# Loading a group's rows two steps before their statistics, taking weight pieces and transform steps by turns, and fetching the remaining rows with six transfers

## The chip, the cores and the metric

The kernel runs on one core of a Trainium2 chip. The core has TensorE (PE, matrix products), VectorE (DVE), ScalarE (ACT), GpSimd (POOL), SyncE (SP, which here only issues transfers) and 16 DMA engines. The metric is the device time of one execution in microseconds. The kernel before takes 1058.84 us, the median of three runs (1058.2 to 1059.17).

## The reference

Three stages follow one another, in float32:

```python
def _attn_ref(q, k, v, tau):                     # batch 4, heads 8, rows 576, head size 64
    scores = scale * np.matmul(q, k.transpose(0, 1, 3, 2))
    thresh = np.max(scores, axis=-1, keepdims=True) - tau
    scores = np.where(scores >= thresh, scores, -1000000000.0)
    ...                                          # softmax over what is left
    return np.matmul(attn, v)

def _moe_ref(x, mu_k, mu_r, w_k, w_v, w_r):      # 4 x 576 x 512, inner size 1024
    xk = mu_k * x + (1.0 - mu_k) * x_prev        # x_prev: x one row later, zeros first
    xr = mu_r * x + (1.0 - mu_r) * x_prev
    k = np.maximum(xk @ w_k, 0.0)
    v = k * k @ w_v
    r = 1.0 / (1.0 + np.exp(-(xr @ w_r)))
    return r * v

def _moe2_ref(x, w_ch1, w_ch2):                  # w_ch1 512 x 2048, w_ch2 2048 x 512
    X = np.fft.fft(x, axis=1)
    X = np.fft.fft(X, axis=2)
    u = x + np.real(X)
    un = (u - mean(u)) / np.sqrt(var(u) + 1e-06)
    return u + np.maximum(un @ w_ch1, 0.0) @ w_ch2
```

The change concerns the third stage.

## The kernel before

The 2304 rows (4 batches of 576) pass the stages as streams that overlap. Attention (to some 508 us) and the second stage (products `kps`, `rps`, `vps`, to some 614 us) work on half a batch at a time. The second stage's output goes through `xnat` to memory as `xd[b]`. The third stage transforms one batch at a time by matrix products with cosine and sine tables, and then runs the two channel products over nine groups of 256 rows.

**Fold.** `fft_fold(b)` loads a batch's rows (`xa`, `xb`, lines 773 and 774; the remaining rows `ra`, `rb` by `load_rem`, lines 777 to 787), and adds and subtracts them in mirrored pairs (`folded`: ACT at lines 792 and 793, DVE at 794 to 797). `ra` holds 98 partitions: the same 32 rows of the batch three times, at partitions 0, 33 and 65, and one more row twice, at 32 and 97; `rb` likewise. A batch takes ten SP transfers for this. **Transform.** `fft_one` and `fft_two` are the products `f` (lines 818 to 821), `fb`, `fz` and `fa`; they store the sum `u` of input and transform as `ud[g]`, two groups for each batch.

**Channel products.** The weights are taken in four quarters. For each group `norm(g)` loads `un` from `ud[g]` (line 995, two transfers of 256 KB), takes mean and variance on DVE (998 to 1009, with a square root on ACT at 1003) and scales on ACT (1011). `turn` transposes it on PE into `ut` (1024), of which ACT writes a high part (1027) and DVE the rest (1028). `ch1` multiplies with `w_ch1` into `c1ps` (1107 to 1109, 12 products of 256 columns for one of four steps f); ACT and DVE make of it the high and low parts `hh` (1119, 1120). `ch2` multiplies with `w_ch2` into `c2ps` (1129 to 1131), and the sum goes into `u` (loaded at 1153, added at 1177, stored at 1178). A later block of `c1ps` takes the buffer of an earlier one once its `hh` is made.

**Weight pieces.** `weight_pieces` loads 256 KB of a weight (`wraw`, line 56, issued on ACT's queue), and DVE and ACT split it into parts for the products (lines 69 to 71, 75, 79). Quarter 1 has 16 pieces.

**The order.** The driver (lines 1233 to 1270) walks over the steps of `mixer()`, (quarter q, group g, step f). For each step it takes so many steps of the generator `behind` as it has credit, two for each of the first groups: in the kernel before all pieces of quarter 1 first, then the transform of batches 2 and 3. `ahead_of` names the group whose `norm` and `turn` are written at step f = 2 of which (q, g). A scheduler then orders each engine's instructions by its own estimate of times and by priorities, so the order in the program is not the order of the code. Transfers issued on SP and ACT share eight semaphores in turn: a transfer waits at its issue until the previous one with its semaphore has landed. The tiles `ra`, `rb`, `un` and `xnat` of the last stream share four buffers of the pool tag "o".

Of the kernel before, what the change touches and what calls it, by code (L numbers as in the profile page):

```python
# [10 lines left out]
F32 = mybir.dt.float32  # L11
# [9 lines left out]
D, FF, FC = 512, 1024, 2048  # L21
# [8 lines left out]
def tile_kernel(ctx: ExitStack, tc: tile.TileContext, a):  # L30
    nc = tc.nc
    pe, dve, act, pool, sp = nc.tensor, nc.vector, nc.scalar, nc.gpsimd, nc.sync
# [5 lines left out]
    xd = [dram.tile([S + 1, D], F32, name=f"xd{b}") for b in range(B)]  # L38
    ud = [dram.tile([128, 2, D], F32, name=f"ud{g}") for g in range(9)]
# [706 lines left out]
    chp = rstack.enter_context(tc.tile_pool(name="chp", bufs=1, side="right"))  # L746
# [30 lines left out]
    def load_rem(b):  # L777

        xa = chp.tile([128, D], F32, tag="o", bufs=4, name="ra")[:98]
        xb = chp.tile([128, D], F32, tag="o", bufs=4, name="rb")[:98]  # L780
        for r in (0, 33, 65):
            sp.dma_start(xa[r:r + 32], xd[b][256:288, :])
            sp.dma_start(xb[r:r + 32], xd[b][544:576, :])
        for r in (32, 97):
            sp.dma_start(xa[r:r + 1], xd[b][576:577, :])
            sp.dma_start(xb[r:r + 1], xd[b][576:577, :])
        return xa, xb

    def folded(xa, xb, n):
# [76 lines left out]
    def fft_fold(b):  # L866
        while written[b] < 2:
            yield
        settle()
        prs = prs_of[b] = load_pairs(b)  # L870
        ra, rb = load_rem(b)
        parts_e, parts_o = [], []
        for xa, xb in prs:
            e, o = folded(xa, xb, 128)
            yield
            parts_e.append(split_tile(e, 257, "fse"))
            parts_o.append(split_tile(o, 256, "fso"))
            yield
        e, o = folded(ra, rb, 98)
        yield  # L880
        ske = stack_tile(e, 257, "ske")
        sko = stack_tile(o, 256, "sko")
        fold_of[b] = (parts_e, parts_o, ske, sko)
        yield

    def fft_one(b):
        parts_e, parts_o, ske, sko = fold_of.pop(b)
        G = [fp.tile([128, 2, 290], F32R, tag=f"G{i}", bufs=1, name=f"G{i}") for i in range(2)]
        Hh = [fp.tile([128, 2, HS], F32R, tag=f"H{i}", bufs=1, name=f"H{i}") for i in range(2)]
        for mc in range(2):  # L890
            o = stage_1(parts_e, ske, tc1, tc1r, 290, 128 * mc, 128 * mc + 128)
            fsplit(G[0][:, mc], G[1][:, mc], o)
            o = stage_1(parts_o, sko, ts1, ts1r, HS, 128 * mc, 128 * mc + 128)
            fsplit(Hh[0][:, mc], Hh[1][:, mc], o)
            yield
        o = stage_1(parts_e, ske, tc1, tc1r, 290, 256, 257)
        fsplit(g1[0:1], g1[32:33], o)
        sl = slice(32 * b, 32 * b + 32)
        act.activation(g1[64:65, sl], o[:, 256:288], AF.Copy)
        dve.tensor_tensor(g1[96:97, sl], o[:, 256:288], g1[0:1, 256:288].bitcast(F32), op=ALU.subtract)  # L900
        for i, x in enumerate((G[0], G[1], Hh[0], Hh[1])):
            act.activation(grem[i][:, :, b, :], x[:, :, 256:288].bitcast(F32), AF.Copy)
        spec[b] = (G, Hh)
        yield

    def fft_two(b):
        G, Hh = spec.pop(b)
        prs = prs_of.pop(b)
        z, _ = stage_2(G, None, 0, 288, 289)
        zr = fp.tile([1, 257], F32, name="zr")  # L910
        act.activation(zr, z[0:1, 0:257], AF.Copy)
        for i in range(2):
            pa, pb = stage_2(G, Hh, 0, 128 * i, 128 * i + 128)
            make_u(2 * b + i, pa, pb, *prs[i], z=zr if i == 0 else None)
            yield
# [12 lines left out]
    def chain(*gens):  # L928
        for g in gens:
            yield from g  # L930


    wq = {}
    SEVEN = (3,)

# [4 lines left out]
    def quarter(q):  # L940

        if q % 2:
            t = [big(f"B{i}", f"cB{i}") for i in range(2)]
            wq[q] = [[x[:, 2048 * k:2048 * k + 2048] for x in t] for k in range(2)]
        else:
            wq[q] = [halves(0, "cA"), None]
        todo = []
        for k, src in enumerate(("w_ch1", "w_ch2")):
            def to(c, n, k=k):
                if wq[q][k] is None:  # L950
                    wq[q][k] = halves(k, "cA")
                return whole(wq[q][k], 2048 * q)(c, n)

            todo += [(a[src], to, 8 * q + j) for j in ((0, 2, 4, 6, 1, 3, 5, 7) if k == 0 else range(8))]
        if q not in SEVEN:
            yield from weight_pieces(todo, None, stage2, 256, rb=3, bb=2, lows=dve if q < 2 else None)
            return
        more[q] = xwp.tile([128, 2, 3, 2, 256], F32R, name=f"more{q}")
        todo = todo[:8] + [(s, to if i % 4 != 1 else lambda c, n: None, 8 * q + i)
                           for (s, to, _), i in zip(todo[8:], (0, 1, 3, 2, 4, 5, 7, 6))]  # L960
        kept = {}

        def less(x, y, to):
            t = spare(F32)
            dve.tensor_tensor(t, x, y, op=ALU.subtract)
            act.activation(to[0], t, AF.Copy)
            pool.tensor_tensor(to[1], t, to[0].bitcast(F32), op=ALU.subtract)
            return t

        def then(k, wf):  # L970
            p, i = divmod(k - 8, 4)
            if k < 8:
                return
            ext = [[more[q][:, p, m, t] for t in range(2)] for m in range(3)]
            if i == 0:
                kept["b11"] = wf
            elif i == 1:
                kept["b12"] = wf
                kept["t1"] = less(wf, kept["b11"], whole(wq[q][1])(1024 * p + 256, 256))
            elif i == 2:  # L980
                less(wf, kept["b12"], ext[1])
                kept["t2"] = less(wf, kept["t1"], ext[0])
            else:
                less(wf, kept["t2"], ext[2])

        yield from weight_pieces(todo, None, stage2, 256, rb=3, bb=2, then=then)


    uts, pairs, hs, more = {}, {}, {}, {}

    def norm(g):

        u = [chp.tile([128, D], F32, tag="o", bufs=4, name="un") for _ in range(2)]
        for j in range(2):
            sp.dma_start(u[j], ud[g][:, j])
        st = chp.tile([128, 32], F32, tag="lnst", bufs=1, name="lnst")
        for j in range(2):
            dve.bn_stats(st[:, 6 * j:6 * j + 6], u[j])
            dve.bn_aggr(st[:, 12 + 2 * j:14 + 2 * j], st[:, 6 * j:6 * j + 6])
        mean, var = st[:, 12:16:2], st[:, 13:16:2]  # L1000
        ve, sd, r0, t0, rstd, nb = (st[:, k:k + 2] for k in (16, 18, 20, 22, 24, 26))
        dve.tensor_scalar(ve, var, 1e-6, None, op0=ALU.add)
        act.activation(sd, ve, AF.Sqrt)
        dve.reciprocal(r0, sd)
        dve.tensor_tensor(t0, r0, r0, op=ALU.mult)
        dve.tensor_tensor(t0, t0, ve, op=ALU.mult)
        dve.tensor_scalar(t0, t0, -0.5, 1.5, op0=ALU.mult, op1=ALU.add)
        dve.tensor_tensor(rstd, r0, t0, op=ALU.mult)
        dve.scalar_tensor_tensor(nb, mean, -1.0, rstd, op0=ALU.mult, op1=ALU.mult)
        for j in range(2):  # L1010
            act.activation(u[j], u[j], AF.Identity, scale=rstd[:, j:j + 1], bias=nb[:, j:j + 1])
        return u
# [191 lines left out]
    for _ in stream:  # L1204
# [9 lines left out]
        if ffn.get("r_done") and len(uts) < 2:  # L1214
            g = len(uts)
# [17 lines left out]
    for _ in cgen:  # L1233
        pass
    behind = chain(
        quarter(1), fft_fold(2), fft_one(2), fft_two(2),
        fft_fold(3), fft_one(3), fft_two(3), fft_last(), done(),
    )

    ahead_of = {(0, 0): 2, (0, 1): 3, (1, 2): 4, (1, 3): 5, (0, 5): 6, (0, 6): 7, (0, 7): 8}  # L1240
    credit = 0.0
    for (q, gs), f in mixer():
        g = gs[-1]
        credit += 2.0 if (q, g) < (0, 4) else 1.25 * len(gs)
        while credit >= 1:
            credit -= 1
            next(behind, None)
        if f == 2 and (q, g) in ahead_of:
            while (q, g) == (0, 5) and not fft_done:
                next(behind)  # L1250
            n = ahead_of[q, g]
            turn(n, norm(n))
        if (q, g) in ((1, 5), (2, 1)) and f == 3:
            for _ in behind:
                pass
            behind = quarter(q + 1)
        if q > 0 and g == 8 and f == 3:
            for _ in behind:
                pass
# [126 lines left out]
```

## Time and profile before

| | |
|---|---|
| median of three runs | 1058.84 us |
| profiled execution | 1057.07 us |
| span of its trace | 1055.0 us |
| TensorE busy | 1004.3 us (95%) |
| VectorE busy | 715.9 us (68%) |
| ScalarE busy | 536.6 us (51%) |
| GpSimd busy | 395.8 us (38%) |
| mean granted clock of TensorE | 0.988 |

TensorE is the engine that is nearly always busy, and 73% of the chain of work that ended last is its own. A share over the whole span says little here: the windows of the stages show where it waited, and the timeline at those places what it waited for. Times of day in the text (as 624.71) are microseconds from the span's start.

### The profile page before, as it was taken

How to read it: one execution, taken by the hardware profiler on the slowest of the kernel's cores; microseconds unless marked ns; L12 is line 12 of the kernel's file. 1: busy time of each engine (PE TensorE's matmuls, PEld its weight loads, DVE VectorE, ACT ScalarE, POOL GpSimd, SP SyncE). 2: the span in 40 equal slices, each digit the busy share in tenths (PEclk: the TensorE clock that was granted, in tenths of full speed). 3: DMA queues.
4: the chain of work that ended last, by engine and by line, in shares of the span. 5: the costliest groups of instructions: out<-in, count | busy, mean ns of one | idle time of the engine just before them, and what ended most of it. 6: DMA issues, size and time to landing. Idle time of an engine off the chain costs nothing.

```text
span 1055.0 us, 18820 instructions
## 1 busy us (share of the span) xinstructions
PE 1004.3 (95%) x6807; PEld 884.6 (84%) x6807; DVE 715.9 (68%) x1880; ACT 536.6 (51%) x1211; POOL 395.8 (38%) x495
## 2 busy tenths in 40 slices
PE   5887889999999999999999988999999999999998
PEld 4565669988998888999799887898998888889997
DVE  6799988667776685865457978556537449236776
ACT  4688767675866757767265734342413113113332
POOL 1545868455574564843233101000014125112231
PEclk9899989999999999999999999999999999999999
DMA  6443331121211212100722656436325435223221
GB/s 223 149 134 86 112 108 60 48 72 38 72 60 54 66 47 72 51 24 14 209 72 88 205 186 200 157 103 226 129 89 184 130 114 179 97 99 122 101 100 61
DMA packets 45636, 114.52 MB, mean 109 GB/s; under 512 B 6319, under 2 KB 6740, under 8 KB 45544
## 3 DMA queue, kind: packets, MB, share of 16 engines
q1 hardware_dynamic: 27920, 74.47, 22.0%
q10 hardware_dynamic: 12344, 22.13, 6.8%
q0 software_dynamic: 5280, 16.72, 4.5%
q8 instruction: 54, 0.88, 0.4%
q14 instruction: 38, 0.31, 0.1%
HBM read 84.98 MB, written 28.32 MB: 107 GB/s over the span
## 4 chain that ended last, share of the span: by engine, by line
PE 73%; DVE 11%; DMA 7%; ACT 4%; issue 3%; POOL 1%; ACTq 0%; SPq 0%; DVEq 0%; POOLq 0%
PE c1ps L1109 6%; PE c1ps L1107 6%; PE c1ps L1108 6%; PE av L388 6%; PE s L227 5%; PE c2ps L1129 4%; PE c2ps L1131 4%; PE c2ps L1130 4%; PE p L1064 4%; PE t L329 4%; PE kps L408 2%; PE vps L536 2%; PE vps L537 2%; PE vps L538 2%; PE kps L409 2%
## 5 line engine op out<-in xcount | busy, mean ns | idle before, releaser
L267 DVE TENSOR_REDUCE small<-s 128x1 f32<-128x576 f32 x144 | 107.0, 752 | 48.1 <-PE s L227 36.9
L1178 POOL DMA_DIRECT2D ud<-u x54 | 29.4, 545 | 268.3 <-DVE u L1177 167.7
L290 POOL TENSOR_SCALAR e<-e,small 128x576 f32<-128x576 f32 x112 | 89.5, 806 | 89.0 <-DVE small L653 74.6
L282 DVE SCALAR_TENSOR_TENSOR e<-s,small,e 128x576 f32<-128x576 f32 x128 | 102.7, 812 | 25.4 <-ACT e L278 22.2
L278 ACT ACTIVATE e<-s,small 128x576 f32<-128x576 f32 x128 | 93.8, 744 | 29.4 <-DVE small L267 27.7
L1119 ACT ACTIVATE hh<-c1ps 128x256 fp32r<-128x256 f32 (+1 forms) x84 | 37.1, 443 | 138.4 <-PE c1ps L1109 114.7
L1120 DVE SCALAR_TENSOR_TENSOR hh<-c1ps,hh 128x256 fp32r<-128x256 f32 (+1 forms) x84 | 41.6, 497 | 86.6 <-ACT hh L1119 86.5
L329 PE MATMUL t<-ident,e 128*128 128x128 f32 x512 | 82.9, 279 | 10.2 <-ACT pt L332 4.6
L332 ACT ACTIVATE pt<-t 128x512 f32<-128x512 f32 x128 | 75.1, 599 | 22.8 <-PE t L329 21.0
L493 POOL TENSOR_TENSOR k<-relu,k 128x288 fp32r<-128x288 f32 x64 | 54.6, 855 | 68.4 <-ACT k L491 64.2
L329 PEld LDWEIGHTS t<-ident,e 128*128 128x128 f32 x512 | 61.6, 142 | 21.3 <-issue 6.5
L408 PE MATMUL kps<-xh,wk 128*128 128x288 f32 x256 | 78.2, 306 | 0.8 <-DVE fdd L851 0.3
L536 PE MATMUL vps<-k,wv 128*128 128x288 f32 x256 | 77.7, 305 | 0.4 <-ACT tg L524 0.4
L537 PE MATMUL vps<-k,wv 128*128 128x288 f32 x256 | 77.4, 303 | 0.0
L538 PE MATMUL vps<-k,wv 128*128 128x288 f32 x256 | 76.8, 301 | 0.0
L1107 PE MATMUL c1ps<-ut,cA 128*128 128x256 f32 (+1 forms) x224 | 71.2, 319 | 5.7 <-DVE hh L1120 4.0
L409 PE MATMUL kps<-xl,wk 128*128 128x288 f32 x256 | 76.3, 298 | 0.0
L410 PE MATMUL kps<-xh,wk 128*128 128x288 f32 x256 | 76.2, 298 | 0.0
L1109 PE MATMUL c1ps<-ut,cB 128*128 128x256 f32 (+1 forms) x256 | 76.0, 297 | 0.0
L1107 PE MATMUL c1ps<-ut,cB 128*128 128x256 f32 (+1 forms) x256 | 75.8, 296 | 0.0
L1108 PE MATMUL c1ps<-ut,cB 128*128 128x256 f32 (+1 forms) x256 | 75.7, 296 | 0.0
L1108 PE MATMUL c1ps<-ut,cA 128*128 128x256 f32 (+1 forms) x224 | 70.8, 316 | 0.2 <-DVE ut L1028 0.2
(273 smaller groups left out, 3117.4 us busy)
## 6 DMA issues: line engine op xcount, KB each, us to landing
u<-ud SPq DMA_DIRECT2D x36, 512.0 KB
wraw<-in_w_ch ACTq DMA_DIRECT2D x64, 256.0 KB
rawqk<-in_qk SPq DMA_DIRECT2D x24, 608.0 KB
ud<-u POOLq DMA_DIRECT2D x54, 256.0 KB, 2.6
v<-in_v SPq DMA_DIRECT2D x16, 320.0 KB
un<-ud SPq DMA_DIRECT2D x18, 256.0 KB
out<-u SPq DMA_DIRECT2D x18, 256.0 KB
wraw<-in_w_k SPq DMA_DIRECT2D x8, 512.0 KB
```

What stands on the lines that cost most here:

```text
L267: dve.tensor_reduce(st[:, 0:1], sps[n][:, :, 0:HS], axis=AX.XY, op=ALU.max, negate=True)
L278: act.activation(two(eview(n)), sps[n][:, :, 0:HS], AF.Exp, bias=st[:, 0:1])
L282: dve.scalar_tensor_tensor(e, sps[n][:, :, 0:HS], st[:, 1:2], e, op0=ALU.is_ge, op1=ALU.mult, accum_out=st[:, 2:3])
L329: pe.transpose(t[:, k, :], e[:, o + 128 * k:o + 128 * (k + 1)], ident)
L408: pe.matmul(ps, wh, x[0][k], start=(k == 0), stop=False)
L409: pe.matmul(ps, wh, x[1][k], start=False, stop=False)
L536: pe.matmul(ps, wv[0][:, c:c + 128], k2[0][:, k, :], start=(k == 0), stop=False)
L537: pe.matmul(ps, wv[0][:, c:c + 128], k2[1][:, k, :], start=False, stop=False)
L538: pe.matmul(ps, wv[1][:, c:c + 128], k2[0][:, k, :], start=False, stop=(k == 7))
L1107: pe.matmul(ps, wh, ut[0][:, k, :], start=(k == 0), stop=False)
L1108: pe.matmul(ps, wh, ut[1][:, k, :], start=False, stop=False)
L1109: pe.matmul(ps, wl, ut[0][:, k, :], start=False, stop=(k == 3))
```

## The change

`load_rem` loads `ra` and `rb` by three transfers each: 64 partitions from one transfer whose source is the same 32 rows read twice (a stride of zero), 32 partitions from another, and the two single rows from a third, whose source is one row read twice. The loads of `un` move out of `norm` into `fetch`, which the driver calls at f = 0 of the same (q, g), and `norm` and `turn` follow at f = 2 (f = 3 for group 2). `by_turns` takes the pieces of quarter 1 and the steps of the transform of batch 2 alternately. Every line behind `by_turns` moves by 17, so `hh` stands at 1136 and 1137 and `bn_stats` at 1015.

```diff
         xa = chp.tile([128, D], F32, tag="o", bufs=4, name="ra")[:98]
         xb = chp.tile([128, D], F32, tag="o", bufs=4, name="rb")[:98]
-        for r in (0, 33, 65):
-            sp.dma_start(xa[r:r + 32], xd[b][256:288, :])
-            sp.dma_start(xb[r:r + 32], xd[b][544:576, :])
-        for r in (32, 97):
-            sp.dma_start(xa[r:r + 1], xd[b][576:577, :])
-            sp.dma_start(xb[r:r + 1], xd[b][576:577, :])
+        for x, r in ((xa, 256), (xb, 544)):
+            rows = xd[b][r:r + 32, :]
+            sp.dma_start(x[33:97], rows.rearrange("(a p) d -> a p d", a=1).to_broadcast([2, 32, D]))
+            sp.dma_start(x[0:32], rows)
+            sp.dma_start(x[32:98:65], xd[b][576:577, :].to_broadcast([2, D]))
         return xa, xb
...
+    def by_turns(*gens):
+        left = list(gens)
+        while left:
+            for g in list(left):
+                try:
+                    next(g)
+                except StopIteration:
+                    left.remove(g)
+                    continue
+                yield
...
+    fetched = {}
+
+    def fetch(g):
+        fetched[g] = [chp.tile([128, D], F32, tag="o", bufs=4, name="un") for _ in range(2)]
+        for j in range(2):
+            sp.dma_start(fetched[g][j], ud[g][:, j])
+
     def norm(g):
 
-        u = [chp.tile([128, D], F32, tag="o", bufs=4, name="un") for _ in range(2)]
-        for j in range(2):
-            sp.dma_start(u[j], ud[g][:, j])
+        if g not in fetched:
+            fetch(g)
+        u = fetched.pop(g)
...
-        quarter(1), fft_fold(2), fft_one(2), fft_two(2),
+        by_turns(quarter(1), chain(fft_fold(2), fft_one(2), fft_two(2))),
...
-        if f == 2 and (q, g) in ahead_of:
+        n = ahead_of.get((q, g))
+        if f == 0 and n:
             while (q, g) == (0, 5) and not fft_done:
                 next(behind)
-            n = ahead_of[q, g]
+            fetch(n)
+        if f == (3 if n == 2 else 2) and n:
             turn(n, norm(n))
```

On SP, where the channel products begin (some 616 us in the kernel before). `ud_67` to `ud_70` are groups 0 to 3, `xd_65` is batch 2. Before:

```order
L1153 DMA u<-ud_67 128x1024
L995 DMA un<-ud_69 128x512
L1153 DMA u<-ud_68 128x1024
L995 DMA un<-ud_69 128x512
L995 DMA un<-ud_70 128x512 x2
L1153 DMA u<-ud_69 128x1024
L782 DMA ra<-xd_65 32x512
L783 DMA rb<-xd_65 32x512
```

After:

```order
L1170 DMA u<-ud_67 128x1024
L783 DMA ra<-xd_65 64x1x512
L784 DMA ra<-xd_65 32x512
L785 DMA ra<-xd_65 2x512
L1170 DMA u<-ud_68 128x1024
L783 DMA rb<-xd_65 64x1x512
L784 DMA rb<-xd_65 32x512
L785 DMA rb<-xd_65 2x512
L1006 DMA un<-ud_69 128x512 x2
L1006 DMA un<-ud_70 128x512 x2
L1170 DMA u<-ud_69 128x1024
```

The remaining rows of batch 2 now go ahead of the loads of groups 2 and 3, which stood around `u1` and ahead of them.

On VectorE, in the same stretch: the rows around the first statistics of group 2. Before:

```order
L69 TENSOR_SCALAR wbits<-wraw 128x256
L70 SCALAR_TENSOR_TENSOR wbits<-wraw,wbits 128x256
L71 SCALAR_TENSOR_TENSOR wbits<-wraw,wbits 128x256
L998 BN_STATS lnst<-un 128x6
L79 TENSOR_TENSOR cB_7703<-wbits,cB_7702 128x256
L1120 SCALAR_TENSOR_TENSOR hh<-c1ps,hh 128x256
L999 BN_AGGR lnst<-lnst 128x2
L79 TENSOR_TENSOR cB_7703<-wbits,cB_7702 128x256
L69 TENSOR_SCALAR wbits<-wraw 128x256
L1120 SCALAR_TENSOR_TENSOR hh<-c1ps,hh 128x256
```

After (the first four `hh` stand ahead of these rows, the fifth is their last):

```order
L79 TENSOR_TENSOR cB_7695<-wbits,cB_7694 128x256
L70 SCALAR_TENSOR_TENSOR wbits<-wraw,wbits 128x256
L793 TENSOR_TENSOR fp<-ra,rb 98x255
L69 TENSOR_SCALAR wbits<-wraw 128x256
L794 TENSOR_TENSOR fq<-rb,ra 98x255
L71 SCALAR_TENSOR_TENSOR wbits<-wraw,wbits 128x256
L1015 BN_STATS lnst<-un 128x6
L70 SCALAR_TENSOR_TENSOR wbits<-wraw,wbits 128x256
L795 TENSOR_TENSOR fy<-fp,fq 98x257
L850 MEMSET fdd 128x1
L1015 BN_STATS lnst<-un 128x6
L1137 SCALAR_TENSOR_TENSOR hh<-c1ps,hh 128x256
```

The statistics (`BN_STATS`) stood ahead of the second `hh`; they now stand behind the fourth and ahead of the fifth, with the fold of the remaining rows (`fp`, `fq`, `fy`) ahead of them.

On TensorE, around the transposes of group 2 (`ut<-ident,un`); `f` is the first transform product of batch 2. Before:

```order
L1130 MATMUL c2ps<-cA_7351,hh 128x512
L1131 MATMUL c2ps<-cA_7350,hh 128x512 x2
L1024 MATMUL ut<-ident,un 128x128 x8
L1129 MATMUL c2ps<-cA_7350,hh 128x512
L1130 MATMUL c2ps<-cA_7351,hh 128x512
L1129 MATMUL c2ps<-cA_7350,hh 128x512
L1130 MATMUL c2ps<-cA_7351,hh 128x512
L1131 MATMUL c2ps<-cA_7350,hh 128x512 x2
L1107 MATMUL c1ps<-ut_7807,cA_7092 128x256 x2
L1108 MATMUL c1ps<-ut_7808,cA_7092 128x256
```

After:

```order
L1147 MATMUL c2ps<-cA_7343,hh 128x512
L1148 MATMUL c2ps<-cA_7342,hh 128x512 x2
L1041 MATMUL ut<-ident,un 128x128 x8
L1124 MATMUL c1ps<-ut_7847,cA_7084 128x256 x2
L817 MATMUL f_7980<-tc_6209,fseh 128x290
L818 MATMUL f_7980<-tc_6209,fseh 128x290
L819 MATMUL f_7980<-tc_6209,fsel 128x290
L817 MATMUL f_7980<-tc_6209,fseh 128x290
L818 MATMUL f_7980<-tc_6209,fseh 128x290
L819 MATMUL f_7980<-tc_6209,fsel 128x290
L820 MATMUL f_7980<-tc1r,ske 128x290
L817 MATMUL f_7990<-ts_6211,fsoh 128x288
```

The six products `c2ps` that followed the transposes now precede them, and 14 products `f` follow, which stood behind the transposes of group 3.

## Rows read from the trace of the kernel before

**Rows 1.** The page: span.

```profile
span 1055.0 us, 18820 instructions
```

**Rows 2.** Windows by stage: length, busy times, granted clock, DMA share, GB/s.

```profile
505.00:560.00 55.00, 52.38 (x380) 48.11 (x379) 28.95 (x69) 24.09 (x73) 18.74 (x29) 1.00 0.53 159
560.00:616.00 56.00, 54.18 (x405) 51.72 (x404) 49.90 (x151) 37.05 (x96) 11.12 (x11) 1.00 0.40 126
616.00:664.00 48.00, 40.66 (x252) 35.97 (x251) 37.84 (x119) 20.07 (x48) 3.42 (x6) 0.96 0.73 228
664.00:1040.00 376.00, 376.00 (x2329) 334.94 (x2328) 213.56 (x482) 104.51 (x226) 78.65 (x103) 1.00 0.38 126
```

**Rows 3.** Timeline of TensorE, 616 to 662 us: start, length, line, idle before.

```profile
624.71 0.58 PE L1107 MATMUL c1ps<-ut,cA 128*128 128x256 f32 x1 [3.84 <-DVE hh L1120]
...
640.63 1.03 PE L1024 MATMUL ut<-ident,un 128*128 128x128 f32 x8
...
647.69 0.50 PE L1129 MATMUL c2ps<-cA,hh 128*128 128x512 f32 x1 [1.31 <-ACT hh L1119]
...
659.32 0.50 PE L1107 MATMUL c1ps<-ut,cA 128*128 128x256 f32 x2 [1.61 <-ACT ut L1027]
```

**Rows 4.** Windows of 4 us inside that stage.

```profile
620.00:624.00 4.00, 0.87 (x4) 0.38 (x2) 0.70 (x2) 0.38 (x1) 0.00 (x0) 1.00 1.03 404
624.00:628.00 4.00, 3.29 (x15) 3.21 (x16) 2.34 (x8) 0.33 (x2) 0.00 (x0) 0.57 0.81 287
```

**Rows 5.** Timeline of TensorE: products at either level of the clock.

```profile
614.27 0.28 PE L1108 MATMUL c1ps<-ut,cA 128*128 128x256 f32 x1
614.39 0.28 PE L1109 MATMUL c1ps<-ut,cA 128*128 128x256 f32 x1
...
620.25 0.39 PE L1129 MATMUL c2ps<-cA,hh 128*128 128x512 f32 x1
620.48 0.39 PE L1130 MATMUL c2ps<-cA,hh 128*128 128x512 f32 x1
...
625.30 0.41 PE L1109 MATMUL c1ps<-ut,cA 128*128 128x256 f32 x1
625.51 0.41 PE L1107 MATMUL c1ps<-ut,cA 128*128 128x256 f32 x1
```

**Rows 6.** Timeline of VectorE, 612 to 662 us.

```profile
623.30 0.69 DVE L998 BATCH_NORM_STATS2 lnst<-un 128x6 f32<-128x512 f32 x1 [4.50 <-DMA un<-ud]
...
624.23 0.42 DVE L1120 SCALAR_TENSOR_TENSOR hh<-c1ps,hh 128x256 fp32r<-128x256 f32 x1
...
630.30 0.69 DVE L998 BATCH_NORM_STATS2 lnst<-un 128x6 f32<-128x512 f32 x1
...
631.65 0.40 DVE L1120 SCALAR_TENSOR_TENSOR hh<-c1ps,hh 128x256 fp32r<-128x256 f32 x1
...
642.77 0.68 DVE L1028 TENSOR_TENSOR ut<-ut,ut 128x512 fp32r<-128x512 f32 x1
```

**Rows 7.** Chain of waits that ended last, 610 to 662 us.

```profile
616.54 6.74 DMA un<-ud
```

**Rows 8.** Timeline of ScalarE and its queue, 612 to 662 us.

```profile
622.61 0.38 ACT L1119 ACTIVATE hh<-c1ps 128x256 fp32r<-128x256 f32 x1 [2.84 <-DMA u<-ud]
```

**Rows 9.** Timeline of ScalarE and its queue, 500 to 532 us.

```profile
522.80 0.33 ACTq L56 DMA_DIRECT2D wraw<-in_w_ch  x1
523.18 0.21 ACT L793 ACTIVATE fq<-xb 128x2 f32<-128x2 f32 x1 [5.58 <-DMA rb<-xd]
...
529.21 0.19 ACT L793 ACTIVATE fq<-rb 98x2 f32<-98x2 f32 x1
```

**Rows 10.** Timeline of SyncE, 500 to 560 us.

```profile
512.47 0.46 SPq L782 DMA_DIRECT2D ra<-xd  x1
```

**Rows 11.** Timeline of TensorE, 505 to 535 us.

```profile
524.81 0.40 PE L818 MATMUL f<-tc,fseh 128*128 128x290 f32 x1 [0.35 <-ACT fseh L803]
```

**Rows 12.** The page: DMA queue, packets, MB, share of 16 engines.

```profile
q1 hardware_dynamic: 27920, 74.47, 22.0%
```

## The prediction

> **What bounds the kernel now.** I read the page first, for the span [rows 1], then the windows by stage [rows 2], since a share over the whole span hides where TensorE stood still. From 664 to 1040 us TensorE is busy 376.00 of 376.00 us: nothing that the change moves can be gained there, only lost. From 505 to 560 it lacks 2.62 us, from 560 to 616 1.82 us, and from 616 to 664, where the channel products begin, 48.00 − 40.66 = 7.34 us. That last stage is the only one with something to win. Its clock is 0.96, not 1.00.
>
> The timeline of TensorE says where the 7.34 us lie [rows 3]: 3.84 us at 624.71 behind a DVE `hh`, 1.31 us at 647.69 behind an ACT `hh`, 1.61 us at 659.32 behind the `ut` of group 3; 0.58 us are left for smaller ones. I then followed the longest one back. DVE stood idle for 4.50 us and then ran the first `bn_stats` of group 2 at 623.30, because `un` had not landed; the `hh` that TensorE needed stands right behind it in DVE's order and runs at 624.23 [rows 6]. The chain of waits names the same transfer: `un`, issued at 616.54 and 6.74 us long [rows 7]. So DVE did no useful work for an instruction that could have waited, at the head of a queue with one that could not. ACT has its own part in it: its `hh` at 622.61 came after 2.84 us in which a weight load ahead of it waited for the semaphore of `u` [rows 8].
>
> The wait has a second price. In the window 620 to 624 TensorE is busy 0.87 of 4 us, and in the next the granted clock is 0.57 [rows 4]. Products of 256 columns then start 0.21 us apart (625.30, 625.51) where they took 0.12 (614.27, 614.39) [rows 5]: near half of the speed, so the lower of the two levels, 1.2 instead of 2.4 GHz. Twelve products at 0.09 us more are 1.1 us; the next ones of 512 columns add about 0.1. The stage has thus 7.34 + 1.2 = 8.5 us that could go at most.
>
> **The order of `hh` and statistics.** In the changed order the first four `hh` stand ahead of both `bn_stats`, and the waits at 624.71 and the fall of the clock should go: −3.84 − 1.2. What is late next I estimate one by one, from the order and the durations above.
>
> The first `hh` now stands behind one weight piece more on DVE: 0.3 us. The second, on ACT, stands behind two weight loads whose semaphores belong to loads issued shortly before; the row nearest to this is the wait of 2.84 us [rows 8], and nothing excludes 0; I take 0.6, nearer to 0, since a weight load has half of `u`'s bytes.
>
> The fifth `hh` is the critical one. Ahead of it on DVE stand `fp` and `fq`, which need the remaining rows of batch 2, and two `bn_stats`, which need both tiles `un`. TensorE without its two losses would be there about 5.0 us (3.84 + 1.2) earlier than before, less the 0.9 just charged. Before, that `hh` ran from 631.65 to 632.05 [rows 6], and between 624.71 and 640.63 TensorE's timeline has no wait [rows 3], so it was asked for at 632.05 or later; 4.1 us earlier that is 628.0 or later, and I take 629.5. If the six transfers of `ra` and `rb` land like other transfers, `un` lands about 4 us later than the 623.28 of before, near 627 to 628, and the `hh` runs at 629.5 to 631. I take 0.9 us of waiting.
>
> The transposes of group 2 stood at 640.63 [rows 3], 10.3 us behind the second `bn_stats` at 630.30 [rows 6]. Now they ask for a `bn_stats` near 629.5, so stand near 640; TensorE comes there near 638.5, with the six `c2ps` products of 0.23 us [rows 5] already done (1.4 us that stood behind before). Wait: 1.5 us. A cover goes with these six: they hid DVE's low half of `ut`, 0.68 us for each of its two pieces [rows 6]; behind the transposes now stand only two `c1ps`. Wait: 0.7 us. For group 3, whose wait was 1.61 us, I take 0.5, since its loads are issued some steps earlier. The wait at 647.69 came from a full ACT queue behind the late weight pieces; with one piece for each transform step I count it as gone.
>
> Sum of what is left: 0.3 + 0.6 + 0.9 + 1.5 + 0.7 + 0.5 = 4.5 us of 8.5, so the stage gains 4.0 us (2.5 if group 2 waits as much as the whole chain allows, 5.5 if `hh` and transposes come free; 8.5 is the ceiling).
>
> **The six transfers.** 16 issues of some 0.46 us [rows 10] leave SP, with the same bytes. SP is on no path by its own time; what counts is the semaphores. From 517.60 to 523.18 ACT stood 5.58 us behind a weight load that waited for the semaphore of one `ra` transfer, issued at 512.47 and landed at about 522.8 [rows 9, 10]. With fewer transfers that load waits for `xb` and an older weight piece instead, which land earlier; ACT's activations behind it start up to 4 us sooner. TensorE felt little of it: 0.35 us at 524.81 behind ACT [rows 11]. Against this the `fq` of the remaining rows, at 529.21 without a wait [rows 9], stands ahead of an activation for the second stage, and now rests on a transfer of a form that the trace does not have. Bounds for 505 to 616: −1.5 (all waits that ACT ends) to +4 (below); I take −0.3.
>
> How long one such transfer of 128 KB takes no row shows. From below: at 404 GB/s [rows 4] 0.33 us beside others. From above: 10.3 us, what the 64 KB of `ra` took while the DMA engines were full [rows 9, 10]. I take the lower end in the stage at 616, since its `un`, four times the bytes of the old row transfer, took 6.7 us [rows 7] with half a megabyte ahead of it, and keep the upper for the range.
>
> Here the row and a rule part. The rows of this kernel show no transfer that reads its source twice. The Trainium skill (DMA: Bandwidth & Descriptors, "Why a DMA increments its semaphore by 16 and not by 1") says that the number of DMA engines is the largest up to 16 that divides the slowest dimension of both sides; with a source of 2 x 32 rows that would be two engines. By it the time would be that of the first rival.
>
> **From 664 us on** the orders grow alike again, near 790 us, and TensorE is full: 0, with up to +1.5 where a weight piece comes late, since the pieces now end later.
>
> **Sum.** −4.0 − 0.3 = −4.3 us against the profiled execution's 1057.07 (its span of 1055.0 and 2.07 around it): 1052.8. The median of the runs is 1.77 above that execution, so 1058.84 − 4.3 = 1054.5 us. Chance 0.50, own range 1052.5 to 1056.5.
>
> **Rival 1: the 64-row transfers crawl on few engines.** On two of them each has 32 packets of 2 KB. The queue's mean is 0.220 x 16 x 1055 / 27920 = 0.133 us for a packet [rows 12], so 4.3 us for each transfer instead of 0.5 over sixteen, and what follows in the queue (`u`, `un`) waits on those two. `rb` then lands near 629 and the fifth `hh` runs near 631.5: 1.8 us more waiting. In the first stage `fq` comes about 2 us late and holds the activation behind it: 2 us. The gain is 4.3 − 1.8 − 2.0 = 0.5: 1058.3. For it: the source's form. Against it: nothing in the trace. Chance 0.26.
>
> **Rival 2: slower.** The same wait for `rb` of batch 0, but at the price of the full engines: a transfer of 64 KB took 10.3 us there [rows 9, 10]. If `rb` lands after 534, ACT stands at `fq` with the activations of the second stage behind it, and TensorE loses one us for each us beyond 530, where it asks for them. At 5 us and a stage at 616 that gains 2.5 it is 1058.84 + 2.5 = 1061.3. It decides from 535 on, where the loss exceeds what the later stage can give. For it: the 10.3 us. Against: only six transfers are issued where ten were, and the last of the ten landed before 529. Chance 0.14.
>
> **Rival 3: the wait moves.** DVE needs 37.84 of 48 us in the stage [rows 2]; if the `bn_stats` chain with the fold's work in it takes 13 us instead of 10.3, the transposes of groups 2 and 3 give back the 3 us: 4.3 − 3 = 1.3, 1057.5. Chance 0.10.
>
> **How the numbers follow.** A measurement of this kernel tells 0.2%, 2.1 us, from no change. Below 1056.7 counts as faster: 0.46 of the forecast's 0.50, 0.06 of rival 1, 0.03 of rival 3: 0.55. Above 1061.0 slower: 0.10 of rival 2, 0.06 of rival 1, 0.03 of late pieces: 0.19. Between them 0.26. The range reaches from 1051 (ceiling nearly reached) to 1061, just short of rival 2.
>
> **What would show it.** Right: no wait above 2 us in TensorE's timeline from 616 to 664, a clock of 1.00 there, idle time of about 4.5 instead of 7.34 us, and the first `bn_stats` of group 2 behind four `hh`. Rival 1: `ra` and `rb` land some 5 us after their issue and the fifth `hh` waits for them. Rival 2: a wait of several us near 530, before a `kps`, that ACT ends. Wrong altogether: a loss after 664, where I count on full cover.

## The result and the profile after

The changed kernel takes 1073.63 us, the median of four runs (1072.77 to 1075.8), beside 1058.52 for the kernel before: a ratio of 1.0145, 95% interval 1.0128 to 1.0163. It is slower by 15 us where 4.3 us of gain were forecast, and lies above the stated range. Ratios here are of undisturbed runs, so they can differ a little from the quotient of the medians beside them.

The page of the changed kernel, its span, TensorE, and the queue that answers to [rows 1, 12]:

```profile
span 1072.3 us, 18786 instructions
...
PE 1010.1 (94%) x6807; PEld 889.7 (83%) x6807; DVE 713.2 (67%) x1880; ACT 535.3 (50%) x1211; POOL 396.5 (37%) x495
...
q1 hardware_dynamic: 27680, 74.47, 21.8%
```

The same 74.47 MB go through the queue. Of the 17.3 us that the span grew, 5.8 are in TensorE's busy time (1004.3 before, with as many instructions: products at the lower clock), the rest is waiting. The windows by stage that answer to [rows 2] (length, busy times with counts, granted clock, DMA share, GB/s):

```profile
505.00:560.00 55.00, 49.25 (x346) 45.04 (x345) 25.90 (x63) 22.70 (x68) 16.68 (x26) 0.97 0.46 138
560.00:616.00 56.00, 52.99 (x387) 50.01 (x386) 47.07 (x141) 35.76 (x97) 13.28 (x14) 1.00 0.46 144
616.00:664.00 48.00, 39.38 (x229) 34.45 (x227) 33.61 (x108) 16.48 (x41) 2.27 (x4) 0.89 0.57 179
664.00:700.00 36.00, 32.75 (x198) 28.72 (x199) 17.42 (x49) 10.88 (x28) 1.08 (x2) 0.91 0.47 145
```

From 505 to 560 TensorE lacks 5.75 us where it lacked 2.62, from 616 to 664 8.62 where it lacked 7.34, and 3.25 us stand after 664, where it had lacked none. All of this is also later by the shift before it, so the sum is better read from the waits themselves, in TensorE's timeline (answering to [rows 3, 11]):

```profile
528.46 0.40 PE L408 MATMUL kps<-xh,wk 128*128 128x288 f32 x1 [2.48 <-ACT xnat L572]
...
531.28 0.66 PE L564 MATMUL xn<-ident,tg 128*128 128x128 f32 x4 [0.96 <-ACT relu L478]
...
532.92 0.40 PE L820 MATMUL f<-tc1r,ske 98*128 98x290 f32 x1 [0.99 <-DVE ske L809]
...
600.09 0.40 PE L408 MATMUL rps<-xr,wr 128*128 128x288 f32 x1 [2.52 <-ACT tg L524]
...
628.75 0.50 PE L1146 MATMUL c2ps<-cA,hh 128*128 128x512 f32 x1 [1.99 <-ACT hh L1136]
...
641.74 0.39 PE L1124 MATMUL c1ps<-ut,cA 128*128 128x256 f32 x1 [2.28 <-DVE hh L1137]
...
653.70 1.36 PE L1041 MATMUL ut<-ident,un 128*128 128x128 f32 x8 [2.22 <-ACT un L1028]
...
668.49 0.58 PE L1124 MATMUL c1ps<-ut,cA 128*128 128x256 f32 x1 [3.25 <-DVE hh L1137]
```

Near 530 there are three waits, 4.43 us together, where the kernel before had 0.35 us behind ACT [rows 11]. At 600.09 there is one of 2.52. In the channel products the wait of 3.84 us is gone, but 1.99, 2.28, 2.22 and 3.25 us are there. ACT's timeline, answering to [rows 8, 9]:

```profile
518.93 0.33 ACTq L56 DMA_DIRECT2D wraw<-in_w_ch  x1
...
527.71 0.21 ACT L791 ACTIVATE fp<-ra 98x2 f32<-98x2 f32 x1 [4.12 <-DMA ra<-xd]
...
530.72 0.21 ACT L792 ACTIVATE fq<-rb 98x2 f32<-98x2 f32 x1 [1.47 <-DMA rb<-xd]
...
628.32 0.66 ACT L1136 ACTIVATE hh<-c1ps 128x256 fp32r<-128x256 f32 x2 [4.41 <-DMA wraw<-in_w_ch]
...
632.00 0.21 ACT L791 ACTIVATE fp<-ra 98x2 f32<-98x2 f32 x1 [2.41 <-DMA ra<-xd]
...
638.17 0.21 ACT L792 ACTIVATE fq<-rb 98x2 f32<-98x2 f32 x1 [4.55 <-DMA rb<-xd]
```

ACT waited 4.12 us at `fp` of `ra` and 1.47 at `fq` of `rb`, with the second stage's activations queued behind both, and again 2.41 and 4.55 us in the later stage. SyncE's timeline says when those tiles were asked for:

```profile
510.05 0.79 SPq L783 DMA_DIRECT2D ra<-xd  x1
...
622.49 0.62 SPq L783 DMA_DIRECT2D ra<-xd  x1
...
631.56 0.62 SPq L783 DMA_DIRECT2D rb<-xd  x1
...
633.72 6.25 SPq L1006 DMA_DIRECT2D un<-ud  x4
```

`ra` of batch 0 was issued at 510.05 and used as it landed, at 527.71: 17.7 us, where 64 KB had taken 10.3 in the same full stretch [rows 9, 10]. In the later stage `ra` was issued at 622.49 and awaited until 632.00, 9.5 us, and `rb` from 631.56 to 638.17, 6.6 us. `un` of group 2 stands behind `rb` on the queue, the first at 633.72. SyncE's own waits in that stage (line, what it waited for, us in total, times, longest) show that `rb` was held until `ra` had landed, and `un` of group 3 until `rb` had:

```profile
SPq L1006 <- DMA rb<-xd: 3.0, 1, 3.0
SPq L783 <- DMA ra<-xd: 3.0, 1, 3.0
```

VectorE has what was forecast, four `hh` ahead of the statistics, and the statistics too late:

```profile
638.19 0.42 DVE L793 TENSOR_TENSOR fp<-ra,rb 98x255 f32<-98x255 f32 x1 [3.55 <-DMA rb<-xd]
...
639.40 0.69 DVE L1015 BATCH_NORM_STATS2 lnst<-un 128x6 f32<-128x512 f32 x1
...
641.28 0.41 DVE L1137 SCALAR_TENSOR_TENSOR hh<-c1ps,hh 128x256 fp32r<-128x256 f32 x1
```

The first `bn_stats`, at 639.40, is later than in the kernel before [rows 6] by 16.1 us, of which 6.3 is the shift that the kernel already had when the channel products began (their first product starts at 613.71 before and at 619.97 now).

The 3.25 us at 668.49 come from batch 3's `ra` by another road, the shared semaphores. It was issued at 654.43 and had not landed before 661.91. A weight load on ACT's queue waited for its semaphore until 661.99, VectorE waited for that weight until 667.40, and the `hh` that TensorE needed stands behind it (ACT's rows, then VectorE's):

```profile
661.99 0.33 ACTq L56 DMA_DIRECT2D wraw<-in_w_ch  x1
...
662.37 0.42 ACT L75 ACTIVATE cB<-wbits 128x256 fp32r<-128x256 f32 x1 [2.19 <-DMA ra<-xd]
...
667.40 0.29 DVE L69 TENSOR_SCALAR wbits<-wraw 128x256 int32<-128x256 int32 x1 [3.11 <-DMA wraw<-in_w_ch]
```

Two windows near 526 show how the DMA engines worked, the first while ACT waited for `ra`, the second while `rb` was still on its way:

```profile
524.00:528.00 4.00, 1.97 (x15) 1.73 (x14) 0.00 (x0) 0.29 (x2) 0.00 (x0) 1.00 0.23 75
527.50:529.00 1.50, 0.54 (x4) 0.55 (x5) 0.00 (x0) 1.21 (x4) 0.00 (x0) 1.00 0.13 52
```

ACT waits for a transfer, and the engines' mean share is 0.23: on average fewer than four of sixteen are at work. From 527.5 to 529.0 no other queue moves anything, and the share of 0.13 is that of two engines, which carry 52 GB/s together.

### The profile page after: what moved, and what is told of

Same layout as the page of the kernel before. It is cut to its first block, busy times and chain, and to the rows that moved or that the text cites. A ratio compares the mean times of both kernels' runs of the same rounds, so it can differ in the third digit from the quotient of the medians.

```text
span 1072.3 us, 18786 instructions
## 1 busy us (share of the span) xinstructions
PE 1010.1 (94%) x6807; PEld 889.7 (83%) x6807; DVE 713.2 (67%) x1880; ACT 535.3 (50%) x1211; POOL 396.5 (37%) x495
## 3 DMA queue, kind: packets, MB, share of 16 engines
q1 hardware_dynamic: 27680, 74.47, 21.8%
## 4 chain that ended last, share of the span: by engine, by line
PE 71%; DMA 10%; DVE 10%; ACT 4%; issue 3%; POOL 2%; SPq 0%; ACTq 0%; DVEq 0%; POOLq 0%
PE c1ps L1124 6%; PE c1ps L1125 6%; PE c1ps L1126 6%; PE av L388 5%; PE s L227 5%; PE c2ps L1148 4%; PE c2ps L1146 4%; PE c2ps L1147 4%; PE p L1081 4%; PE t L329 3%; PE kps L408 2%; DMA rawqk<-in_qk 2%; PE vps L536 2%; PE vps L537 2%; PE kps L409 2%
```

## The experiments

Three theories stood against one another. A: the 64-row transfer runs on two DMA engines, because its source has an outer dimension of two. B: reading the same rows twice is slow by itself. C: the new order of pieces, transform and statistics costs the time, and the transfer is beside the point.

**The same order, another number of blocks.** Three kernels differ from the changed one in the source of the 64-row transfer alone, and their instructions stand in the same order on every engine. They read other rows than the result needs.

```diff
-            sp.dma_start(x[33:97], rows.rearrange("(a p) d -> a p d", a=1).to_broadcast([2, 32, D]))
+k16         sp.dma_start(x[33:97], rows[0:4].rearrange("(a p) d -> a p d", a=1).to_broadcast([16, 4, D]))
+k4          sp.dma_start(x[33:97], rows[0:16].rearrange("(a p) d -> a p d", a=1).to_broadcast([4, 16, D]))
+apart       sp.dma_start(x[33:97], xd[b][r - 96:r + 32, :].rearrange("(a p) d -> a p d", a=2)[:, 32:64])
```

> The changed kernel with one size changed: the 64-row transfer reads 4 rows sixteen times (source 16 x 4 rows, stride 0) in place of 32 rows twice; same bytes, same order on every engine; 60 of its 64 rows are other rows than the reference wants. Theory A (a transfer runs on as many DMA engines as divide the outer dimension of both sides, here 16 where the changed kernel has 2): the transfer lands about 2 to 3 us after its issue when the engines are free, not 6 to 9; the waits of ACT and VectorE on ra and rb go, and the time falls from 1073.6 to between 1054 and 1061. Theory B (a source read again is slow by itself): as slow as the changed kernel or slower, 1072 or more. Theory C (the order by turns and the early loads cost the time, the transfer is beside the point): 1068 to 1073.

> The same with a source of 4 x 16 rows, stride 0: same bytes and order, 32 of the 64 rows are other rows. Theory A: four engines, 16 packets on each instead of 32, so the transfer takes about half of the changed kernel's, and the time lies between the two, 1060 to 1067. Theory B: 1073. Theory C: 1068 to 1073.

> The changed kernel with a source of 2 x 32 rows that lie 64 rows apart: two different blocks, no row read twice, same bytes and order (32 of the 64 rows are other rows). Theory A (two engines because the outer dimension is 2): as slow as the changed kernel, 1071 to 1076. Theory B (reading the same rows twice is what is slow): like 16 x 4 rows or better, 1057 to 1062.

| source of the 64 rows | median us | ratio to before, 95% interval |
|---|---|---|
| 2 x 32, rows read twice (the change) | 1073.63 | 1.0145, 1.0128 to 1.0163 |
| 2 x 32, two different blocks (apart) | 1072.14 | 1.0136, 1.0101 to 1.0171 |
| 4 x 16 (k4) | 1063.28 | 1.0045, 1.0030 to 1.0060 |
| 16 x 4 (k16) | 1060.1 | 1.0015, 1.0003 to 1.0027 |

B falls twice: two different blocks are as slow as one block read twice, and one block read sixteen times is the fastest. C falls for the larger part: with the same order 13.8 us go away (1.0145 − 1.0015 of 1058.5), to within some 2 us. The 1.6 us that are left, for the order, are less than the 0.2% that a measurement tells from none. What matters is the outer dimension. ACT's timeline near 530 in the kernel with two different blocks, then in the one with four, then with sixteen:

```profile
527.22 0.21 ACT L791 ACTIVATE fp<-ra 98x2 f32<-98x2 f32 x1 [3.50 <-DMA ra<-xd]
...
530.12 0.21 ACT L792 ACTIVATE fq<-rb 98x2 f32<-98x2 f32 x1 [1.35 <-DMA rb<-xd]
```

```profile
525.99 0.21 ACT L791 ACTIVATE fp<-ra 98x2 f32<-98x2 f32 x1 [0.89 <-DMA ra<-xd]
...
529.79 0.21 ACT L792 ACTIVATE fq<-rb 98x2 f32<-98x2 f32 x1 [2.25 <-DMA rb<-xd]
```

```profile
523.04 0.20 ACT L791 ACTIVATE fp<-ra 98x2 f32<-98x2 f32 x1
...
524.53 0.19 ACT L792 ACTIVATE fq<-rb 98x2 f32<-98x2 f32 x1
```

The wait for `ra` is 3.50 us with two blocks (4.12 in the changed kernel), 0.89 with four and none with sixteen; the waits for both tiles sum to 4.85 (5.59), 3.14 and none. The Trainium skill (DMA: Bandwidth & Descriptors, "Why a DMA increments its semaphore by 16 and not by 1") gives two, four and sixteen engines for these sources; the order of the four times agrees with it. The traces show the number too. They record when parts of a transfer report that they have landed: all eight 64-row transfers report two parts with two blocks, read twice or different, four parts with four blocks and sixteen with sixteen (with fewer than sixteen there is one more mark some 1.1 us after the issue, long before the data). The share of 0.13 above says two engines as well.

The same records show what the two engines do to the transfers behind. The 32-row transfer of `ra` that the changed kernel issues at 511.81 has fourteen of its sixteen parts by 519.54, and the last two at 527.20 and 527.43, right behind the two parts of the 64-row transfer (527.01 and 527.21). The first `un` of group 2 has fourteen by 637.40 and the last two at 638.84 and 639.09. The records don't name the engines, but two late parts of sixteen each time fit the two that are still at work on the 64-row transfer.

From issue to its last part a 64-row transfer takes 9.6 us on the mean of the eight in the changed kernel, 7.6 with four blocks and 5.5 with sixteen. What the form adds is 4.0 us on the mean (1.6 to 6.7); the rest is what the queues cost any form at these places.

**Which stage pays.** The rows read twice for batches 0 and 1 alone:

```diff
-            sp.dma_start(x[33:97], rows.rearrange("(a p) d -> a p d", a=1).to_broadcast([2, 32, D]))
+            sp.dma_start(x[33:97], (rows if b < 2 else rows[0:4]).rearrange("(a p) d -> a p d", a=1)
+                         .to_broadcast([2, 32, D] if b < 2 else [16, 4, D]))
```

> The changed kernel with the 32 rows read twice for batches 0 and 1 only; for batches 2 and 3 it reads 4 rows sixteen times (same bytes and order; their rows are other rows). It splits the 13.5 us between the changed kernel (1073.6) and the one with 16 x 4 rows throughout (1060.1). If both stages pay about what the traces show by the start of the first c1ps (7.2 us of it by 614): 1066 to 1069. If the loss is all in the channel products: 1060 to 1062. If all of it is in the early folds: 1072 to 1074.

1063.97 us, 1.0061 (1.0042 to 1.0079). By the ratios, of the 13.8 us between the changed kernel and `k16` 4.9 belong to the first two batches (the waits near 530, 4.43 us in the trace, agree) and 8.9 to the other two, each to within some 2 us. That lies between the ranges of the expectation, which put more into the early stage. Its 7.2 us were the distance of two traces at the first channel product, 619.97 in the changed kernel and 612.78 in `k16`. In the trace of this kernel, with the same early transfers, the product starts at 617.77, 5.0 us behind `k16`: a pair of single traces gives that part to some 2 us and no better.

**The parts of the change alone.** The six transfers in the kernel before; turns and early loads with the ten old transfers; turns alone; early loads alone:

```diff
rem_only     load_rem of the change in the kernel before, nothing else
turns_fetch  the change with load_rem of the kernel before
turns_only   -        quarter(1), fft_fold(2), fft_one(2), fft_two(2),
             +        by_turns(quarter(1), chain(fft_fold(2), fft_one(2), fft_two(2))),
fetch_only   fetch(n) at f == 0, norm and turn at f == 2 or 3, nothing else
```

> The kernel before with the six transfers alone (old order of pieces and transform, loads of un as before). Theory A: the losses near 528 (some 4 us) and those around the channel products come with the transfer alone: 1064 to 1072. Theory C: 1057 to 1060.

> The changed kernel with the ten old transfers of a batch: turns and early loads alone. Theory A: the stage at 616 gains what was predicted or part of it, 1054 to 1058. Theory C: 1068 or more.

> The kernel before with pieces and transform by turns alone. Turns and early loads together gave 1061.0 with waits of 3.02 behind an ACT hh, 1.81 and 4.15 us for group 2. If the turns cost it (weight pieces of quarter 1 and the fold share DVE and the stores' semaphores): 1060 to 1064. If the early loads cost it: 1057 to 1059.

> The kernel before with the loads of un at f = 0 and norm at f = 2 or 3 alone. If moving the first statistics behind hh is what removes the 3.84 us and the fall of the clock, this alone gains 2 to 5 us: 1053.5 to 1056.5. If the scheduler puts the statistics ahead of hh anyway: 1058 to 1060.

| kernel | median us | ratio to before, 95% interval |
|---|---|---|
| six transfers alone | 1067.6 | 1.0077, 1.0058 to 1.0096 |
| turns and early loads | 1061.0 | 1.0028, 1.0014 to 1.0042 |
| turns alone | 1061.0 | 1.0027, 1.0013 to 1.0040 |
| early loads alone | 1059.01 | 1.0002, 0.9988 to 1.0015 |

The transfers cost most by themselves, as A says. Turns and early loads together lie above A's range and below C's. The order by turns costs some 3 us with the ten old transfers where I had forecast 4 us of gain, and the early loads alone do nothing: in their kernel the first statistics still stand ahead of the second `hh`, and TensorE waits as before [rows 3]:

```profile
627.60 0.39 PE L1125 MATMUL c1ps<-ut,cA 128*128 128x256 f32 x1 [3.89 <-DVE hh L1138]
```

With the turns that wait is gone from VectorE and is found at ACT, and the wait before the transposes of group 2 is new. TensorE's timeline with the turns alone, then ACT's:

```profile
622.16 0.50 PE L1140 MATMUL c2ps<-cA,hh 128*128 128x512 f32 x1 [2.65 <-ACT hh L1130]
...
636.46 0.50 PE L1140 MATMUL c2ps<-cA,hh 128*128 128x512 f32 x1 [1.48 <-DVE u L1188]
...
646.66 1.97 PE L1035 MATMUL ut<-ident,un 128*128 128x128 f32 x8 [4.15 <-ACT un L1022]
```

```profile
621.44 0.24 ACTq L576 DMA_DIRECT2D xd<-xnat  x1
...
621.73 0.38 ACT L1130 ACTIVATE hh<-c1ps 128x256 fp32r<-128x256 f32 x1 [4.65 <-DMA wraw<-in_w_ch]
```

ACT's second `hh` stands behind the last store of `xnat`, which waits at its issue for the semaphore of a weight load: 4.65 us idle, of which TensorE feels 2.65. And the remaining rows now go ahead of `un` of group 2, so that its scaling is late by 4.15 us. The three waits sum to 8.28 us; the kernel before had 7.34 in all of the stage.

**Mending the transfer.** The 64 rows as two transfers of 32, eight a batch, in the changed kernel and in the kernel before; and the same two with the stores of the last `xnat` on GpSimd's queue:

```diff
-            sp.dma_start(x[33:97], rows.rearrange("(a p) d -> a p d", a=1).to_broadcast([2, 32, D]))
-            sp.dma_start(x[0:32], rows)
+            for p in (33, 65, 0):
+                sp.dma_start(x[p:p + 32], rows)
...
-                            act.dma_start(xd[b][r0:r0 + tn, :], n[:tn])
+pool                        (pool if last else act).dma_start(xd[b][r0:r0 + tn, :], n[:tn])
...                          # and the store of the single row behind it likewise
```

> The changed kernel with the 64-row transfer cut into two of 32 rows (eight transfers a batch, each of its large ones divisible by 16). Theory A (the number of DMA engines follows from the outer dimension): no wait of several us for ra or rb is left; like the kernel with 16 x 4 rows, 1057 to 1062, because the order by turns keeps a second wait of ACT behind the stores of xnat. Theory C2 (fewer issues on SP are worth something by themselves): under 1056.

> The kernel before with eight transfers a batch instead of ten, none with its source read twice except the two single rows (4 KB). Theory A: no loss such as the six transfers alone showed (1067.6); 1057 to 1059.5. If a smaller number of transfers shifts the semaphores for the worse: 1062 or more.

> The changed kernel with eight transfers a batch (1056.8) and, besides, the stores of the last stream's xnat issued by GpSimd and not by ACT. If ACT's second hh is held by those stores (the 3.0 or 5.0 us seen with the order by turns), that wait goes: 1053 to 1056. If it only moves to the next late thing (statistics of group 2): 1056 to 1059.

> The kernel before with eight transfers a batch (1055.6) and the same stores on GpSimd. If the first 3.84 us near 624 come from un alone, the stores change nothing: 1055 to 1057. If they hold ACT there: 1052 to 1055.

| kernel | median us | ratio to before, 95% interval |
|---|---|---|
| change with eight transfers | 1056.79 | 0.9986, 0.9970 to 1.0001 |
| before with eight transfers | 1055.6 | 0.9982, 0.9968 to 0.9996 |
| change with eight, stores on GpSimd | 1058.96 | 1.0004, 0.9990 to 1.0018 |
| before with eight, stores on GpSimd | 1060.11 | 1.0016, 0.9997 to 1.0035 |

Eight transfers of a plain shape are the only part that gains: the kernel before with these alone is the fastest here, by 0.18%, with an interval below 1 but no more than the 0.2% that a measurement tells from none; I had expected no gain of it. With the whole change around them the time is the same within the intervals, between the two ranges of its expectation. So the 3 us that the turns cost with ten transfers are not seen with eight: what the parts cost does not add up. The stores on GpSimd take ACT's wait away and give nothing. TensorE with eight transfers, then with the stores moved as well:

```profile
622.55 0.79 PE L1146 MATMUL c2ps<-cA,hh 128*128 128x512 f32 x1 [3.60 <-ACT hh L1136]
...
643.03 1.36 PE L1041 MATMUL ut<-ident,un 128*128 128x128 f32 x8 [0.72 <-ACT un L1028]
```

```profile
631.08 0.50 PE L1146 MATMUL c2ps<-cA,hh 128*128 128x512 f32 x1 [0.82 <-DVE u L1194]
...
642.89 1.97 PE L1041 MATMUL ut<-ident,un 128*128 128x128 f32 x8 [5.75 <-ACT un L1028]
```

VectorE's second `bn_stats` of group 2 in the latter:

```profile
632.08 0.68 DVE L1015 BATCH_NORM_STATS2 lnst<-un 128x6 f32<-128x512 f32 x1
```

The 3.60 us at the second `hh` are gone, and the transposes of group 2 wait 5.75 instead of 0.72: TensorE comes earlier to a chain of statistics that isn't earlier. That is the wait of the prediction's third rival, in a kernel without the slow transfer, but not its cause: from the second `bn_stats` to the transposes it takes 10.8 us, near the 10.3 of before, and not 13. The kernel before with the stores on GpSimd is slower than without them, outside both ranges of its expectation; why was not followed up.

## Why the prediction was wrong

**The step that failed is the price of the transfer.** "I take the lower end in the stage at 616, since its `un`, four times the bytes of the old row transfer, took 6.7 us [rows 7] with half a megabyte ahead of it." The row is of a transfer with 128 rows on both sides; the new one has another form, and for that form no row stood. The lower end was 0.33 us beside others; the measured time from issue to use is 9.5 and 6.6 us there and 17.7 in the first stage, above even the upper end of 10.3. The form is worth 13.8 us in all, the difference between two kernels of one order.

**The mechanism was in the prediction as the first rival, and its price for one transfer was near.** It had 4.3 us instead of 0.5 for each, 3.8 more; measured are 4.0 more on the mean. Its sign was seen as well: the fifth `hh` waits for `rb`, and TensorE with it for 2.28 us at 641.74, where it had 1.8. What it had wrong is what the delays cost TensorE: 1.8 + 2.0 us in all, for 1058.3, where 13.8 are measured. Four things are missing in that sum. It charged batch 0 for `rb` alone, where `ra` is the first to hold ACT. In the later stage `rb` was issued only when `ra` had landed, and `un` behind both, so two delays add. Batch 3 was not charged, and its `ra` held a weight load (the 3.25 us at 668.49). And the clock fell again behind the new waits: the stages above show 0.97, 0.89 and 0.91 where [rows 2] have 1.00, 0.96 and 1.00.

The second rival had the right place for the early stage, ACT with the second stage's activations queued behind the remaining rows. That its 5 us are near the 4.9 measured is luck. It counted on `rb` landing after 534 and on one us lost for each us beyond 530; `fq` of `rb` ran at 530.72, which gives 0.7. The longest of the three waits, 2.48 us at 528.46, ended with an `xnat` that stands behind `fp` of `ra`. This rival also lacked the larger loss in the later stage, which I had left as a gain of 2.5.

The clock behind the wait of 1.99 us at 628.75, in windows of 4 us of the changed kernel (answering to [rows 4]):

```profile
628.00:632.00 4.00, 3.25 (x13) 2.97 (x14) 2.48 (x7) 1.27 (x5) 0.00 (x0) 0.67 0.80 266
632.00:636.00 4.00, 4.00 (x25) 3.67 (x24) 1.29 (x4) 0.89 (x3) 0.00 (x0) 0.90 0.73 231
```

**The second step that failed is the gain of 4.0 us in the channel products.** The order did what I read from it: the second to fourth `hh` no longer stand behind the statistics. But waits that I estimated one by one were too small. The second `hh` on ACT was put at 0.6 us, "nearer to 0"; it cost 2.65, 2.57 and 3.60 us in three kernels with the turns. The row of 2.84 us [rows 8] was the better guide, and I argued it away by the bytes of a load. What ACT waits for is the landing of an earlier transfer, whose semaphore the last store of `xnat` takes over: a weight load with the turns alone, an earlier store of `xnat` with `k16` and with eight transfers. The transposes of group 2 were put at 1.5; they cost 4.15 with ten transfers, 1.59 with `k16` and 0.72 with eight. The kernel with `k16`, which has the forecast's order and a 64-row transfer on sixteen engines, shows the whole of it. TensorE's timeline, then the window of its stage (its first channel product starts 0.9 us earlier than in the kernel before):

```profile
592.88 0.40 PE L408 MATMUL rps<-xr,wr 128*128 128x288 f32 x1 [2.52 <-ACT tg L524]
...
622.15 0.78 PE L1146 MATMUL c2ps<-cA,hh 128*128 128x512 f32 x1 [2.57 <-ACT hh L1136]
...
642.36 1.36 PE L1041 MATMUL ut<-ident,un 128*128 128x128 f32 x8 [1.59 <-ACT un L1028]
...
644.65 0.50 PE L1124 MATMUL c1ps<-ut,cA 128*128 128x256 f32 x2 [0.93 <-ACT ut L1044]
...
645.83 0.41 PE L817 MATMUL f<-tc,fseh 128*128 128x290 f32 x1 [0.68 <-DVE ut L1045]
...
615.00:663.00 48.00, 41.01 (x243) 36.01 (x242) 35.59 (x114) 19.67 (x48) 2.27 (x4) 0.93 0.70 220
```

The cover that went with the six `c2ps` was put at 0.7 and cost 0.93 and 0.68; the fifth `hh`, put at 0.9, cost nothing. TensorE lacks 48.00 − 41.01 = 6.99 us there (in a profiled execution 2.6 us under this kernel's median), against the 4.5 forecast and the 7.34 before. And the clock is 0.93 where it had been 0.96, so the 1.2 us that the prediction took back from the clock are not gained either. The 2.52 us at 592.88 were in no sum of mine: the scaling of `un` stands there ahead of the second stage's `tg` on ACT, as in the changed kernel, and TensorE waits for `tg`. With ten transfers (turns alone) and with eight the wait of that stretch is 0.95 us. The order there had moved with the number of transfers, and I hadn't compared it.

**What was right.** The early activations on ACT did start sooner: the weight load that had waited until 522.80 [rows 9] is issued at 518.93. The wait of 3.84 us behind the statistics goes with the turns. That nothing can be gained after 664 holds as well. That something is lost there was the prediction's own sign of being wrong altogether, and it was seen: 3.25 us at 668.49, with a clock of 0.91 from 664 to 700. In `k16` TensorE has no wait between 655 and 760, so that loss too belongs to the slow transfer.

## What to carry to other kernels

Fewer transfers aren't cheaper if one of them has a form that few engines carry. Before merging transfers, look at the outer dimension of both sides: two blocks of 32 rows and two transfers of 32 rows are not the same thing. When the one term with no row in the trace is also the one that others queue behind, its price is a chain and not a single landing; the forecast is then that of the chain's upper end, or there is none. A wait taken from the head of one engine's queue is gained only up to the next late thing, here ACT's second `hh` and the scaling of group 2.

## What the runs showed of the hardware

The form of a source decided more than its bytes or its repetition. Against 128 KB as 16 x 4 rows, read sixteen times, the same bytes as 2 x 32 rows cost 13.8 us over eight transfers, and as 4 x 16 rows 3.2. They report two, four and sixteen parts landed. A transfer of sixteen parts behind one of two parts had fourteen of them 7.7 us before the last two.

While two slow transfers were under way, the mean share of the DMA engines fell to 0.23 with a consumer waiting: a low share is no sign that transfers don't bind.
